# Loading the slopes earlier, holding the decay tables in the shared slots and re-timing the preparation of weights

## The chip, the cores and the metric

One core of a Trainium2 chip runs one launch. The time is device microseconds of that core, the median of several executions. Engines are named as in the profile: PE is TensorE, PEld its weight loads, DVE is VectorE, ACT is ScalarE, POOL is GpSimd, SP is the engine whose queue issues the DMAs.

## The reference

```python
# q, k, v: 4 x 8 heads x 576 x 64
gamma = 1 - 2 ** (-5 - arange(8))
D[i, j] = gamma ** (i - j) if i >= j else 0
x = (((q @ k.T) / 8) * D) @ v            # retention, heads joined: 2304 x 512
h = x @ w_in                             # 512 x 2048
x = (max(h, 0) + alpha * min(h, 0)) @ w_out
out = (sigmoid(x @ w_gate) * (x @ w_val)) @ w_out2   # 512 x 1536, 1536 x 512
```

All of it in float32. `alpha` holds one slope for each of the 2048 hidden columns: 8 KB.

## The kernel before

The 2304 tokens are cut into five blocks (256 and four times 512), and the sequences into 25 runs of up to 128 tokens (chunks); runs 0 and 1 fill block 0, runs 2 to 6 block 1. Each product is made of three matmuls, from operands that are split into a high and a low part (`split`: ACT copies the high part, DVE subtracts).

**Attention.** For each run, POOL multiplies q by a decay table (`att_q`) and v by per-row factors (`att_v`), PE makes the scores `s`, DVE masks them (`sc`, `qk`), PE makes the output `o` and the state update `m`, DVE adds to the state `m_sb`, and ACT and DVE split `o` into `x`. The decay table of a run that does not start a sequence is made by four ACT copies (`dec`, L266) in a pool of two buffers of its own. PE's scores of a run take over the PSUM tiles of an earlier one, so they wait until that one's `x` is split.

**Weights.** A weight block arrives as 64-bit words (`r`, L142, 512 KB), and `prepare_weight` turns it into high and low parts: two ACT rescales (L153, L155), three DVE operations (L159, L160, L163), an ACT copy (L170) and a DVE subtraction (L172). A load is asked for when an earlier block is begun; the first four at the start. `weight_step(n)` adds n to a credit, begins one more weight at each whole credit, and emits one further stage of each weight under way. `PACE_B` is n in the attention runs from `WITH` on, four steps a run; `PACE_C` in the joint steps (L505 to L523), where block 0 and most of block 1 go through the first feed-forward layer, four or five steps for each hidden block f; `PACE_E` in the last block, where the second layer's weights are begun; `PACE_F` in the second layer.

**Slots.** Tiles of 4 KB per partition share a pool of `NSLOT` slots: loaded q, k and v, raw and prepared weights, activations `g`. All 32 weights of the first layer stay until the last block.

**Order.** PE's instructions run in the order written. Those of ACT, DVE, POOL and SP are ordered by a planner that gives each engine the earliest-written instruction that it takes to be ready; on the chip each engine then runs its list in that fixed order. `alpha` is loaded (L481) after the loads of the first seven runs, and L482 makes its negative, `na_sb`, which the slope of the first layer (L410) reads while weights are still being prepared.

The last line of a block of layer 1 (`drain`) copies its four sums from PSUM by way of two staging tiles (`yst`) to HBM; the next block's sums take over the PSUM tiles.

Of the kernel before, what the change touches and what calls it, by code (L numbers as in the profile page):

```python
# [9 lines left out]
F32 = mybir.dt.float32  # L10
# [3 lines left out]
AF = mybir.ActivationFunctionType  # L14
# [4 lines left out]
P = 128  # L19
B, H, S, D = 4, 8, 576, 64  # L20
NPAIR = H // 2
# [5 lines left out]
BLOCKS = (256, 512, 512, 512, 512)  # L27
FIRST = tuple(sum(BLOCKS[:j]) for j in range(len(BLOCKS)))
NBLK = len(BLOCKS)
NSLOT = 38  # L30

ORDER = (1, 2, 3, 4, 0)

# [8 lines left out]

BEHIND = 2

WITH = 3


PACE_B, PACE_C, PACE_E, PACE_F = 0.34, 0.5, 0.65, 1


def chunks():
# [39 lines left out]
def retention_two_ffn(ctx: ExitStack, tc: tile.TileContext, att, cst, alpha, w1, w2, out):  # L91
    nc = tc.nc

    const = ctx.enter_context(tc.tile_pool(name="const", bufs=1))

    big = ctx.enter_context(tc.tile_pool(name="big", bufs=NSLOT))
    xp = ctx.enter_context(tc.tile_pool(name="xp", bufs=2))
# [8 lines left out]
    ap = att_only.enter_context(tc.tile_pool(name="ap", bufs=1))  # L106
    c_sb = ap.tile([P, N_CST], F32, tag="c", name="c_sb")
    al_sb = const.tile([P, NF1], F32, tag="al", name="al_sb")
    na_sb = const.tile([P, NF1], F32, tag="na", name="na_sb")
# [6 lines left out]
    def slot(shape, dtype, name):  # L116
        return big.tile(shape, dtype, tag="big", name=name)
# [66 lines left out]
    def load_weights(n):  # L184
        for key in to_load[:n]:
            load_weight(key)
        del to_load[:n]

    def advance():

        for g in list(under_way):
            if next(g, StopIteration) is StopIteration:
                under_way.remove(g)

    def begin_weight():
        if to_prepare and to_prepare[0] in raw_w:
            under_way.append(prepare_weight(to_prepare.pop(0)))
            load_weights(1)

    def weight(*key):  # L200
        while key not in wt:
            begin_weight()
            advance()
        return wt[key]
# [3 lines left out]
    def weight_step(n):  # L208

        credit[0] += n  # L210
        if credit[0] >= 1.0:
            credit[0] -= 1.0
            begin_weight()
        advance()
# [9 lines left out]
    def load_chunk(n):  # L224
        if n >= len(CHUNKS) or n in raw_a:
            return
        load_qk(n)
        load_kv(n)
# [28 lines left out]
    def att_q(n):  # L257

        _, _, pos, c, _ = CHUNKS[n]
        by = decay  # L260
        if pos:

            by = ap.tile([P, NPAIR, P], F32, tag="dec", name=f"dec{n}", bufs=2)
            for pr in range(NPAIR):
                g = O_GP + STARTS.index(pos) * NPAIR + pr
                nc.scalar.activation(by[:, pr, :c], decay[:, pr, :c], AF.Copy, scale=c_sb[:, g:g + 1])  # L266
        for part in (slice(0, 2), slice(2, 4)) if n == 0 else (slice(0, 4),):
            q = raw_a[n][0][:, 0, part, :c]
            nc.gpsimd.tensor_tensor(out=q, in0=q, in1=by[:, part, :c], op=ALU.mult)  # L269
# [66 lines left out]
    def runs_of(j):  # L336
        return [n for n, ch in enumerate(CHUNKS) if ch[0] == j]
# [6 lines left out]
    def att_stages(j):  # L344

        for n in runs_of(j):
            x_of(n)
            s_sb = att_scores(n, ps_a, "ab")
            load_qk(n + 1)
            yield  # L350
            att_values(n, s_sb, ps_a, "ab")
            load_kv(n + 1)
            if n + 1 < len(CHUNKS):
                att_q(n + 1)
                att_v(n + 1)
            yield

    def att_run(runs, pools, pace, fill):

        scored = []  # L360

        def score(i):
            if i < len(runs):
                n = runs[i]
                x_of(n)
                pool = pools[i % len(pools)]
                scored.append((n, att_scores(n, *pool), *pool))
                if i + 1 < len(runs):
                    att_q(n + 1)
                    att_v(n + 1)  # L370

        def weights(i):
            weight_step(pace(i))
            weight_step(pace(i))

        att_q(runs[0])
        att_v(runs[0])
        score(0)
        for i in range(len(runs)):
            weights(i)  # L380
            att_values(*scored[i])
            fill(i)
            weights(i)
            if i == 0:
                score(1)
            score(i + 2)
# [14 lines left out]
    def ffn1_h(j, f):  # L401
        w = weight(1, f, 0)
        nb = BLOCKS[j]
        ps = ps_h.tile([P, nb], F32, tag="h", name=f"h{j}_{f}")
        products(ps, [(cols(w, k), x_t[j][:, :, k]) for k in range(KC)])
        t = small.tile([P, nb], F32, tag="t", name=f"t{j}_{f}", bufs=1)
        if to_prepare:
            nc.scalar.activation(t, ps, AF.Relu)
            nc.scalar.activation(ps, ps, AF.Relu, scale=-1.0)
            nc.vector.scalar_tensor_tensor(ps, ps, na_sb[:, f:f + 1], t, ALU.mult, ALU.add)  # L410
        else:
            nc.vector.tensor_scalar(t, ps, 0.0, al_sb[:, f:f + 1], ALU.min, ALU.mult)  # L412
            nc.vector.scalar_tensor_tensor(ps, ps, 0.0, t, ALU.max, ALU.add)  # L413
        name = f"g{j}_{f}"
        g_t[j, f] = slot([P, 2, nb], F32R, name) if nb > DM // 2 else half_of_slot(name)
        split(g_t[j, f][:, 0], g_t[j, f][:, 1], ps)
# [31 lines left out]
    def load_x2(j, k):  # L448
        if k == 0:
            x2_t[j] = new_x(j, "x2_")  # L450
        st = small.tile([P, BLOCKS[j]], F32, tag="st", name=f"x2r{j}_{k}")
        nc.sync.dma_start(out=st, in_=x2d[j][:, k, :])
        split(x2_t[j][:, 0, k], x2_t[j][:, 1, k], st)
# [24 lines left out]
    nc.gpsimd.memset(m_sb, 0.0)  # L478
    for n in runs_of(0) + runs_of(1):
        load_chunk(n)  # L480
    nc.sync.dma_start(out=al_sb, in_=alpha)  # L481
    nc.scalar.activation(na_sb, al_sb, AF.Copy, scale=-1.0)  # L482
    load_weights(4)

    pa, py = (ps_a, "ab"), (ps_y, "yy")
# [1 line left out]
    done = [0]  # L487

    def first_h(i):
        while done[0] < EARLY and done[0] * (n0 + n1 - LATE) < EARLY * (i + 1 - LATE):  # L490
            ffn1_h(0, done[0])
            done[0] += 1
# [3 lines left out]
    def later(n):  # L496

        while len(late) > n:
            ffn1_y(*late.pop(0))


    att_run(runs_of(0) + runs_of(1), [pa, py, py], lambda i: PACE_B if i >= WITH else 0, first_h)
    weight(1, 0, 1)

# [19 lines left out]
    n = runs_of(2)[0]  # L524
# [3 lines left out]
    for j in range(1, NBLK):  # L528
        stages = att_stages(j + 1) if j + 1 < NBLK else iter(())
        first = step1 if j == 1 else 0  # L530
        total = 2 * len(runs_of(j + 1))
        span = SPAN * (NF1 - first) // NF1
        staged = 0
        if j == NBLK - 1:
            att_only.close()
            extra.append(ctx.enter_context(tc.tile_pool(name="extra", bufs=NEXTRA)))
        for f in range(first, NF1):
            ffn1_h(j, f)
            if j == NBLK - 1:
                if f == 0:  # L540
                    to_load += [(2, f2, m) for f2 in range(NF2) for m in range(3)]
                    to_prepare += to_load
                    load_weights(3)
                if 8 <= f < 8 + KC:
                    load_x2(ORDER[0], f - 8)
                weight_step(PACE_E)
            for point in range(2):
                if staged < total and staged * span < total * (2 * (f - first) + point):
                    next(stages)
                    staged += 1  # L550
                if point == 0:
                    later(BEHIND - 1)
                    if j == NBLK - 1:
                        weight_step(PACE_E)
            late.append((j, f))
        for _ in stages:
            pass
# [58 lines left out]
```

## Time and profile before

| | |
|---|---|
| median of 3 executions | 947.21 us (946.84 to 948.40) |
| profiled execution | 946.92 us, of which the span of its instructions 945.1 us |
| mean granted TensorE clock | 0.993 |
| busy PE / PEld | 915.4 us (97%) / 769.2 us |
| busy DVE / ACT / POOL | 429.8 / 310.8 / 45.1 us |
| attention runs 0 to 6 | to about 50 us |
| joint steps | about 50 to 155 us |
| rest of layer 1, attention of the other runs | to about 493 us |
| layer 2 | to the end |

In a row of the timeline the first number is the start, the second the duration, `x16` a count of instructions merged, and the bracket holds the engine's idle time before it and what ended it. A granted clock of 1.00 is 2.4 GHz, 0.50 is 1.2 GHz. Times are microseconds from the start of the span.

### The profile page before, as it was taken

Reading aid. Unit: us, or ns where it says so; the run is one execution under the profiler, and the core shown is the slowest. Engines: PE = TensorE matmul, PEld = TensorE weight load, DVE = VectorE, ACT = ScalarE, POOL = GpSimd, SP = SyncE. Lnnn points to the kernel's source line nnn. Section 1 sums busy time; section 2 is a strip of 40 time slices with the busy share of each in tenths; the row PEclk is TensorE's granted clock in tenths of the full one; section 3 lists DMA queues with packets and bytes.
Section 4 is the critical chain, followed back from the end, with each engine's and each line's share of the span. In section 5 each row is a group of like instructions: output and inputs, shape, how many; then the busy total and the mean of one; then the engine's idle time right before and its main releaser. Section 6 shows DMA issues by size and latency. Waiting matters only on the chain.

```text
span 945.1 us, 12323 instructions
## 1 busy us (share of the span) xinstructions
PE 915.4 (97%) x5032; PEld 769.2 (81%) x5032; DVE 429.8 (45%) x726; ACT 310.8 (33%) x604; POOL 45.1 (5%) x46
## 2 busy tenths in 40 slices
PE   6689999999999999999999999999999999999998
PEld 5578888888888888878888888888888888888897
DVE  2989974454443544378787831321122112211212
ACT  3588942221111111157776631211122111211211
POOL 6000001111000000000000000000000000000000
PEclk9799999999999999999999999999999999999999
DMA  9932302332010210145443500200020001000100
GB/s 323 362 100 83 109 23 90 131 103 69 23 57 24 90 45 23 45 160 181 150 155 123 167 1 0 89 1 1 1 74 16 1 1 48 19 1 1 45 1 23
DMA packets 27976, 69.86 MB, mean 74 GB/s; under 512 B 6928, under 2 KB 8464, under 8 KB 27920
## 3 DMA queue, kind: packets, MB, share of 16 engines
q1 hardware_dynamic: 27920, 69.08, 21.6%
q8 instruction: 39, 0.64, 0.3%
q14 instruction: 17, 0.14, 0.0%
HBM read 59.64 MB, written 9.44 MB: 73 GB/s over the span
## 4 chain that ended last, share of the span: by engine, by line
PE 87%; DVE 6%; ACT 3%; DMA 1%; issue 1%; SPq 1%; DVEq 0%; ACTq 0%
PE z L396 31%; PE h L396 18%; PE y L396 17%; PE o L396 16%; PE s L287 1%; DVE r L160 1%; DVE r L163 1%; PE o L326 1%; PE o L306 1%; DVE w L172 1%; ACT r L153 1%; ACT r L155 1%; SPq L253 1%; DMA al_sb<-alpha 1%; DVE h L410 1%
## 5 line engine op out<-in xcount | busy, mean ns | idle before, releaser
L396 PE MATMUL z<-x,w 128*128 128x512 f32 (+1 forms) x1440 | 305.4, 368 | 0.0
L396 PEld LDWEIGHTS z<-x,w 128*128 128x128 f32 x1440 | 252.4, 188 | 45.8
L396 PE MATMUL h<-x,w 128*128 128x512 f32 (+1 forms) x960 | 213.7, 372 | 6.9 <-DVE g L132 5.4
L396 PEld LDWEIGHTS h<-x,w 128*128 128x128 f32 x960 | 167.3, 190 | 39.4 <-DVE g L132 6.4
L396 PE MATMUL y<-g,w 128*128 128x512 f32 x768 | 186.8, 392 | 1.9 <-ACT yst L423 1.9
L396 PEld LDWEIGHTS y<-g,w 128*128 128x128 f32 x768 | 143.2, 188 | 33.4 <-ACT yst L423 2.3
L396 PE MATMUL o<-w,p 128*128 128x512 f32 x648 | 156.8, 389 | 0.0
L463 DVE TENSOR_TENSOR z<-sg,z 128x512 f32<-128x512 f32 (+1 forms) x60 | 38.5, 642 | 258.3 <-PE z L396 258.3
L396 PEld LDWEIGHTS o<-w,p 128*128 128x128 f32 x648 | 120.9, 188 | 24.5
L131 ACT ACTIVATE g<-h 128x512 fp32r<-128x512 f32 (+1 forms) x80 | 44.3, 554 | 199.1 <-DVE h L413 183.0
L462 ACT ACTIVATE sg<-z 128x512 f32<-128x512 f32 (+1 forms) x60 | 33.2, 553 | 169.1 <-PE z L396 168.9
L131 ACT ACTIVATE p<-z 128x512 fp32r<-128x512 f32 (+1 forms) x60 | 33.3, 555 | 132.5 <-DVE z L463 132.5
L412 DVE TENSOR_SCALAR t<-h,al_sb 128x512 f32<-128x512 f32 (+1 forms) x43 | 31.5, 733 | 99.1 <-PE h L396 99.1
L132 DVE TENSOR_TENSOR g<-h,g 128x512 fp32r<-128x512 f32 (+1 forms) x80 | 50.8, 635 | 24.7 <-ACT g L131 22.2
L132 DVE TENSOR_TENSOR p<-z,p 128x512 fp32r<-128x512 f32 (+1 forms) x60 | 38.3, 638 | 33.2 <-ACT p L131 33.1
L160 DVE CUSTOM_DVE_ANT_0 r<-r,t 128x1024 uint16<-128x1024 uint16 x68 | 46.6, 689 | 4.7 <-ACT g L131 0.5
L163 DVE SCALAR_TENSOR_TENSOR r<-r 128x512 uint32<-128x512 uint32 x68 | 46.7, 686 | 0.5
L172 DVE TENSOR_TENSOR w<-r,w 128x512 fp32r<-128x512 f32 x68 | 45.2, 685 | 3.3 <-ACT w L170 3.2
L153 ACT ACTIVATE r<-r 128x512 f32<-128x512 f32 x68 | 45.7, 672 | 1.1 <-DMA r<-w 1.1
L155 ACT ACTIVATE r<-r 128x512 int32<-128x512 uint32 x68 | 45.8, 674 | 0.0
L170 ACT ACTIVATE w<-r 128x512 fp32r<-128x512 f32 x68 | 43.5, 668 | 3.3 <-PE o L396 2.6
L287 PE MATMUL s<-qk 64*128 64x128 f32 (+1 forms) x320 | 24.2, 293 | 10.8 <-POOL qk L269 6.4
(46 smaller groups left out, 506.2 us busy)
## 6 DMA issues: line engine op xcount, KB each, us to landing
r<-w SPq DMA_DIRECT2D x68, 512.0 KB, 3.7
kv<-att SPq DMA_DIRECT2D x16, 512.0 KB, 3.6
qk<-att SPq DMA_DIRECT2D x15, 512.0 KB, 3.9
y<-ost SPq DMA_DIRECT2D x18, 256.0 KB, 2.0
x2d<-yst SPq DMA_DIRECT2D x16, 256.0 KB, 2.3
x2r<-x2d SPq DMA_DIRECT2D x16, 256.0 KB, 2.9
qk<-att SPq DMA_DIRECT2D x6, 256.0 KB, 4.1
kv<-att SPq DMA_DIRECT2D x4, 256.0 KB, 6.2
```

Of the source, the lines that this page charges most:

```text
L131: nc.scalar.activation(hi, src, AF.Copy)
L132: nc.vector.tensor_tensor(out=lo, in0=src, in1=hi.bitcast(F32), op=ALU.subtract)
L153: nc.scalar.activation(high.bitcast(F32), high.bitcast(F32), AF.Copy, scale=2.0 ** -112)
L155: nc.scalar.activation(low.bitcast(I32), low, AF.Copy, scale=2.0 ** -29)
L160: nc.vector.tensor_tensor(out=low.bitcast(I32), in0=low.bitcast(I32), in1=top.bitcast(I32), op=ALU.add)
L163: nc.vector.scalar_tensor_tensor(low, high, 0x80000000, low, ALU.bitwise_and, ALU.bitwise_or)
L170: nc.scalar.activation(w[:, 0, :], low.bitcast(F32), AF.Copy)
L172: nc.vector.tensor_tensor(out=w[:, 1, :], in0=low.bitcast(F32), in1=w[:, 0, :].bitcast(F32), op=ALU.subtract)
L287: nc.tensor.matmul(ps[e][:c, pr, :c], qk[r, 1, pr, :c], qk[r, 0, pr, :c], start=True, stop=True)
L396: nc.tensor.matmul(ps, l, r, start=first and i == 0, stop=last and i == len(todo) - 1)
L462: nc.scalar.activation(t, ps[0], AF.Sigmoid)
L463: nc.vector.tensor_tensor(out=ps[1], in0=t, in1=ps[1], op=ALU.mult)
```

## The change

`alpha` is asked for right after the first run's loads, and its negative is written where the first hidden block of block 0 begins. The decay tables come from the shared slots, which grow from 38 to 39 (two buffers of 2 KB give way to one slot of 4 KB). Weights are begun from the fifth attention run on instead of the fourth, and at 0.62 instead of 0.5 for a step in the joint steps. In the last block of layer 1 the second layer's weights are begun from the third hidden block on; their first three loads stay where they are.

```diff
-NSLOT = 38
+NSLOT = 39
...
-WITH = 3
+WITH = 4
+LATER = 2
-PACE_B, PACE_C, PACE_E, PACE_F = 0.34, 0.5, 0.65, 1
+PACE_B, PACE_C, PACE_E, PACE_F = 0.34, 0.62, 0.65, 1
...
-            by = ap.tile([P, NPAIR, P], F32, tag="dec", name=f"dec{n}", bufs=2)
+            by = slot([P, NPAIR, P], F32, f"dec{n}")
...
     for n in runs_of(0) + runs_of(1):
         load_chunk(n)
-    nc.sync.dma_start(out=al_sb, in_=alpha)
-    nc.scalar.activation(na_sb, al_sb, AF.Copy, scale=-1.0)
+        if n == 0:
+            nc.sync.dma_start(out=al_sb, in_=alpha)
     load_weights(4)
...
     def first_h(i):
+        if i == 0:
+            nc.scalar.activation(na_sb, al_sb, AF.Copy, scale=-1.0)
         while done[0] < EARLY and done[0] * (n0 + n1 - LATE) < EARLY * (i + 1 - LATE):
...
                     load_x2(ORDER[0], f - 8)
-                weight_step(PACE_E)
+                if f >= LATER:
+                    weight_step(PACE_E)
...
                     later(BEHIND - 1)
-                    if j == NBLK - 1:
+                    if j == NBLK - 1 and f >= LATER:
                         weight_step(PACE_E)
```

`first_h(i)` is called behind the output products of run i of the attention (`fill` in `att_run`).

## Rows read from the trace of the kernel before

**Rows 1.** Waits of PE: microseconds in total, times, longest.

```profile
PE h L396 <- DVE g L132: 5.4, 5, 1.9
...
PE o L306 <- DVE m_sb L320: 3.7, 1, 3.7
```

**Rows 2.** Timeline of ACT, 12 to 38 us.

```profile
23.28 0.22 ACT L482 ACTIVATE na_sb<-al_sb 128x16 f32<-128x16 f32 x1 [4.21 <-DMA al_sb<-alpha]
...
24.57 0.64 ACT L153 ACTIVATE r<-r 128x512 f32<-128x512 f32 x1
...
25.67 0.57 ACT L131 ACTIVATE x<-o 128x512 fp32r<-128x512 f32 x1
```

**Rows 3.** Timeline of PE, 12 to 30 us.

```profile
18.69 0.27 PE L326 MATMUL o<-sc,kv 128*64 128x128 f32 x1
...
27.28 0.82 PE L287 MATMUL s<-qk 64*64 64x64 f32 x14 [4.40 <-DVE x L132]
```

**Rows 4.** Timeline of DVE, 14 to 34 us.

```profile
25.24 0.43 DVE L159 TENSOR_SCALAR t<-r 128x512 uint32<-128x512 uint32 x1 [6.24 <-ACT r L153]
...
30.81 0.84 DVE L320 TENSOR_TENSOR m_sb<-m_sb,m 64x256 f32<-64x256 f32 x2
```

**Rows 5.** Timeline of SP's queue, the issues of loads from 16 us on.

```profile
16.52 0.58 SPq L481 DMA_DIRECT2D al_sb<-alpha  x1
17.15 12.39 SPq L142 DMA_DIRECT2D r<-w  x13
```

**Rows 6.** DMA issues at 16.5 and 17.15 us: KB, microseconds from issue to landing.

```profile
al_sb<-alpha SPq DMA_DIRECT2D x1, 8.0 KB, 6.7
...
r<-w SPq DMA_DIRECT2D x1, 512.0 KB, 7.1
```

**Rows 7.** Busy time by stretch, then granted clock, DMA share and GB/s.

```profile
24.57:50.33 25.76, 17.05 (x207) 15.00 (x207) 24.64 (x50) 15.70 (x32) 0.00 (x0) 0.80 0.86 337
50.33:87.00 36.67, 35.51 (x206) 31.31 (x207) 32.64 (x61) 29.69 (x61) 0.00 (x0) 1.00 0.28 90
87.00:113.72 26.72, 24.06 (x156) 21.73 (x155) 26.72 (x53) 24.41 (x51) 0.00 (x0) 1.00 0.34 114
113.72:134.40 20.68, 19.07 (x113) 16.93 (x114) 17.96 (x33) 13.99 (x28) 0.00 (x0) 1.00 0.08 26
```

The columns are the stretch, its length, and the busy time (instructions) of PE, PEld, DVE, ACT and POOL.

**Rows 8.** Timeline of PE at the start of the last block of layer 1.

```profile
419.17 2.07 PE L396 MATMUL y<-g,w 128*128 128x512 f32 x6 [1.89 <-ACT yst L423]
```

**Rows 9.** Busy time by stretch, as in Rows 7, behind that wait.

```profile
420.20:423.60 3.40, 3.40 (x9) 2.63 (x8) 3.40 (x7) 1.90 (x4) 0.00 (x0) 0.50 0.70 220
```

**Rows 10.** Timeline of ACT, 402 to 425 us.

```profile
418.49 0.63 ACT L423 ACTIVATE yst<-y 128x512 f32<-128x512 f32 x1
```

**Rows 11.** Timeline of PE in the joint steps, 122 to 160 us.

```profile
123.60 1.60 PE L396 MATMUL h<-x,w 128*128 128x256 f32 x12
126.81 3.02 PE L396 MATMUL h<-x,w 128*128 128x512 f32 x12 [1.61 <-DVE g L132]
...
133.82 4.35 PE L396 MATMUL h<-x,w 128*128 128x256 f32 x24
...
154.82 2.91 PE L396 MATMUL h<-x,w 128*128 128x512 f32 x12
```

**Rows 12.** Costliest groups of DVE, 25 to 134 us, shapes apart: busy us, mean ns.

```profile
L132 DVE TENSOR_TENSOR g<-h,g 128x256 fp32r<-128x256 f32 x13 | 5.4, 418 | 0.0
```

**Rows 13.** Timeline of SP's queue, 157 to 172 us.

```profile
166.94 0.33 SPq L253 DMA_DIRECT2D kv<-att  x1
```

**Rows 14.** Timeline of PE, 155 to 400 us, scores.

```profile
169.75 1.16 PE L287 MATMUL s<-qk 64*128 64x128 f32 x16
```

**Rows 15.** Timeline of POOL and ACT, 140 to 172 us: a table's use, a table.

```profile
161.89 1.29 POOL L269 TENSOR_TENSOR qk<-qk,dec 128x512 f32<-128x512 f32 x1 [12.26 <-DMA qk<-att]
...
163.22 1.28 ACT L266 ACTIVATE dec<-c_sb 128x128 f32<-128x128 f32 x4 [3.32 <-POOL qk L269]
```

**Rows 16.** Waits of ACT, as in Rows 1.

```profile
ACT r L153 <- DMA r<-w: 1.1, 2, 0.6
```

## The prediction

> **What bounds the kernel now.** I read first the busy shares, then PE's waits, then the timelines of the engines that those waits name, then busy time by stretch. PE is busy 915.4 of 945.1 us, so all that can be had is some 30 us, and they lie in three places.
>
> The first is the attention of the first seven runs. PE stands still for 4.40 us before a run's scores and for 3.7 us before an `o` product [rows 1, 3]. The scores wait for an `x` whose matmuls had ended at 18.69 + 0.27 = 18.96, while ACT copied it only at 25.67 [rows 2, 3]. What is to be seen on ACT: it stood idle 4.21 us in front of `na_sb`, which waited for `alpha`, and behind that came the rescales of the first weight, and only then the `x` [rows 2]. DVE sat idle 6.24 us for the same rescale and did the state update that the `o` product wants at 30.81 [rows 4]. `alpha` was issued at 16.52, right before the first weight's load at 17.15 [rows 5]; they landed 6.7 and 7.1 us later, at 23.2 and 24.25 [rows 6]. So two late landings stand one behind the other in ACT's list, 1 us apart.
>
> The second is the joint steps. From 24.57 to 134.40, where the last weight of layer 1 is ready, DVE works 24.64 + 32.64 + 26.72 + 17.96 = 101.96 of 109.83 us, and from 87.00 to 113.72 all the time [rows 7]. PE's five waits for a `g` (5.4 us) are DVE's lateness [rows 1]. So up to 134 us DVE sets the pace as much as PE.
>
> The third is the start of layer 1's last block: 1.89 us of waiting for a drain [rows 8], behind which the granted clock is at its lower level, 0.50, from 420.2 to 423.6 [rows 9]; half of those 3.4 us is lost, 1.7. The drain itself, on ACT, starts at 418.49 [rows 10], between rescales of the second layer's weights.
>
> **The change part by part.** *Slopes early.* `alpha`'s load moves past twelve loads of SP's queue, six of q and k and six of k and v. Its issue takes 0.58 us [rows 5], so that each could be 0 to 0.58 us late. I take 0: loads wait some 7 us between issue and landing [rows 6], and the queue stays full. The 0.22 us of `na_sb` [rows 2] move to a place where ACT has time, 20 us before its first reader. What does it bring? It takes 4.21 us of idleness from ACT, but the next entry of ACT's list, the first weight's rescale, can't start before 24.25. The weight is written two runs behind the `x` and was put ahead of it all the same; nothing in the change tells the planner that the load will be late, and the start at the fifth run moves the written place, not the landing. If that order stays, the `x` starts at 24.25 + (25.67 - 24.57) = 25.35 instead of 25.67: 0.3 us. The bounds are 0.3 us and, if the attention goes first, all of DVE's 6.24 idle us [rows 4].
>
> *Weights from the fifth run on, and 0.62 a step.* Nothing is added: the same 32 weights, in another order. What the order does is a sum over DVE. Before, sixteen steps of 0.34 begin five weights in the attention (5.44); the other 27 want (27 - 0.44) / 0.5, so 54 joint steps, and three more until the last is ready: the 57th, with the end of hidden block 11. After, twelve steps begin four (4.08); 28 want 27.92 / 0.62, so 46, and three: the 49th, right behind the second product of hidden block 10. So the last weight is ready sooner as PE counts. PE's work between those places is from 123.60 to the end of the first half of the product at 133.82, about 135.3, less a wait of 1.61: 10.1 us [rows 11]. DVE's share in it is the six operations of three activations, at 0.42 us for 256 columns and up to twice that for 512 [rows 12]: 2.5 to 3.4, taken as 2.8.
>
> DVE must do 101.96 - 2.8 = 99.2 us before that place, from 24.57 - 0.3 = 24.3 on, with X idle: 123.5 + X. PE then has 10.1 + (154.82 - 135.3) = 29.6 us without DVE's load to the end of the joint steps, at 153.1 + X, against 154.82. Bounds of X: the 1.1 idle us of the first stretch alone, or all 7.9 [rows 7]. More weights stand ready, which fills the 4.0 idle us from 50.33 to 87.00; of the 2.7 of the last stretch, where weights run out, I keep 1.5. X = 2.6, and the joint steps end 0.9 us later: beginning more weights early only puts more of DVE's work in front of PE's activations, and PE has more left to do when it is over. Bounds -0.6 and +6.2. What hides the weights is PE's own work; where DVE is full that cover is gone, and the activations queued behind a weight's four operations are late next, then PE's next `h`.
>
> *Decay tables in slots.* ACT no longer waits for the table before last, but a table now needs a slot of the shared pool, and asks behind the next run's k and v. Those were issued at 166.94, when the slots of the run before came free at the end of its `o` products [rows 13]; the 39th slot now serves them earlier, and the table takes what comes free at 166.9. The next scores started at 169.75 [rows 14]. In between must lie the `x` copy (0.57), a table (1.28) and POOL's product (1.29) [rows 2, 15]: 166.9 + 3.1 = 170.0, 0.3 us late. That tightness holds for two runs of block 2; the later blocks have more between runs. I take +0.5, bounds 0 and, at 0.4 for each of eleven later tables, 4.4.
>
> *Later start of layer 2's weights.* Three hidden blocks' worth of steps less in front of the drains: the wait of 1.89 and the 1.7 of lower clock go, 3.6 [rows 8, 9]. The loads stay, so rescales can still fill ACT's gaps; bounds 0 and -3.6, taken -3.6. Some 2.6 weights fewer are ready when layer 2 begins, against about 18 that are; that costs nothing.
>
> The sum: +0.9 + 0.5 - 3.6 = -2.2 on the profiled execution's 946.92 (span 945.1 and 1.8 around it), so 944.7; its median over runs is 947.21, 0.3 above, so 945.0. A change below 0.2%, 1.9 us, can't be told from none here.
>
> **The rivals.** *The attention goes first.* With the tables made early and `alpha` there, the planner may put `x`, masks and state updates ahead of the first weight. Then DVE fills its 6.24 us of idleness with some seven operations of 0.6 us, 4.4 us: 940.6. For it: all inputs lie ready at 18.96. Against it: the planner put the weight first with the `x` older. It decides if the `x` precedes L153.
>
> *The joint steps cost more.* If the extra weights don't fill DVE's gaps, X is 7.9: 945.0 + 5.3 = 950.3, slower than before. Its place is `h` behind `g`, 5.4 us before; it decides from about 10 us on. For it: DVE is full already; against it: four of the idle us lie where weights were lacking.
>
> *The drain stays late*, since the first loads and so their rescales are where they were: the change does not do what it says: 945.0 + 3.6 = 948.6. For it: a rescale fills any gap of ACT that the planner sees; against it: the drains are now written ahead of all but those three.
>
> *Tables late in every run:* 945.0 - 0.5 + 4.4 = 948.9; for it the two rows at 166.94 and 169.75, against it the longer spacing later.
>
> *The slot is what lacked.* If PE's waits for `g` came from loads that had no slot, the 39th would give 5.4 us back instead of losing 0.9: 938.7. Against it: ACT waited for a raw weight only 1.1 us in all [rows 16]. The Trainium skill, Perfetto Trace Analysis, "Optimization Strategy", says that a gap repeating on the engine that should be full can mean that the next tile has no room in SBUF or PSUM; by that rule the extra slot would be the gain here, and this trace does not agree, with DVE and not a load named before all five waits.
>
> **How the numbers follow.** Chances: the forecast 0.40 (own range 942.5 to 947.5), attention first 0.19, joint steps dearer 0.17, drain late 0.12, tables late 0.08, slot 0.04. Faster, below 945.3, takes 0.22 of the forecast, all but 0.01 of the second case and the slot: 0.44. Slower, above 949.1, takes 0.01 of the forecast, 0.13 of the third case, 0.05 of the drain's and 0.04 of the tables': 0.23. The rest, 0.33, is the same. The range 938.5 to 950.5 leaves out the far tails of the second and the third, where idle time of both ends meets the other terms' bounds, less than 0.2.
>
> **What would show it.** In the new trace: no wait of ACT for `alpha`, but one for the first weight, with the `x` behind it near 25.4 (or near 19, then the second case); the joint steps' end near 155.7 and `h` behind `g` above 6 us; DVE full from 50 to 110; no wait for a drain in the last block and a clock of 1.00 around it; scores in block 2 a few tenths late. I am wrong if the order on ACT turns, or if PE waits for DVE little in spite of a full DVE.

## The result, and the profile after

The changed kernel takes 955.49 us (median of 4, 954.09 to 955.91) against 947.81 for the kernel before, run beside it: ratio 1.0084 (95% interval 1.0070 to 1.0098), 7.7 us slower. The profiled execution, the quickest of the four, took 954.09 us, its span 952.3. Lines of the changed kernel are two further on (L396 is L398), L410 to L413 included; the copy of a `yst` is L425 and `na_sb` L493.

Where the time goes is read best as a race between the two traces, by the start of the same PE instruction:

| PE starts | before | after | later by |
|---|---|---|---|
| first `h` of block 0 | 42.36 | 43.09 | 0.7 |
| second product, hidden block 0 (`y0a`) | 55.7 | 56.6 | 0.9 |
| the same, hidden block 4 | 85.3 | 88.0 | 2.7 |
| hidden block 6 | 97.5 | 105.8 | 8.3 |
| hidden block 9 | 119.3 | 130.7 | 11.4 |
| end of the joint steps (`h`) | 154.82 | 164.36 | 9.5 |
| layer 2 | 493.0 | 500.2 | 7.2 |
| end | 945.1 | 952.3 | 7.2 |

So most of the loss is made between 85 and 130 us; 1.9 us come back by the end of the joint steps and some 2.4 more before layer 2. PE's waits after, as in [rows 1] (microseconds in total, times, longest):

```profile
PE s L289 <- POOL qk L271: 10.1, 5, 5.4
PE h L398 <- DVE g L134: 7.8, 5, 3.5
PE o L308 <- DVE m_sb L322: 5.9, 2, 3.9
PE h L398 <- ACT w L172: 2.2, 2, 1.8
PE h L398 <- DVE w L174: 0.9, 2, 0.6
```

PE waits 7.8 us for a `g` instead of 5.4, and newly 3.1 us for weights (`w`). The wait of 4.4 us for an `x` [rows 3] is down to 0.3 and the one for a `yst` [rows 8] is gone. But the waits for POOL's `qk` grew from 6.4 to 10.1 us and those for the state `m_sb` from 4.3 to 5.9, so the attention ends no sooner for it. The start, on ACT's timeline, as in [rows 2]:

```profile
8.40 0.22 ACT L493 ACTIVATE na_sb<-al_sb 128x16 f32<-128x16 f32 x1 [6.39 <-DMA al_sb<-alpha]
8.52 4.80 ACT L268 ACTIVATE dec<-c_sb 128x128 f32<-128x128 f32 x17
...
23.91 0.67 ACT L155 ACTIVATE r<-r 128x512 f32<-128x512 f32 x1 [9.40 <-DMA r<-w]
...
26.04 0.70 ACT L155 ACTIVATE r<-r 128x512 f32<-128x512 f32 x1 [0.90 <-DMA r<-w]
...
27.18 0.61 ACT L133 ACTIVATE x<-o 128x512 fp32r<-128x512 f32 x1
```

The slopes' negation is now the first entry of ACT's list; it waits 6.39 us for `alpha` and holds the tables until 8.52. Later the first weight's rescale stands in front of the `x`, as forecast, but a second weight's rescale does too: the `x` is copied at 27.18, not 25.35. PE's timeline in the joint steps, three of its eight rows with a wait, as in [rows 11], and then the busy time by stretch, as in [rows 7] and [rows 9]:

```profile
59.96 0.50 PE L398 MATMUL h<-x,w 128*128 128x256 f32 x2 [1.78 <-ACT w L172]
...
97.67 5.49 PE L398 MATMUL h<-x,w 128*128 128x512 f32 x12 [3.32 <-DVE g L134]
...
123.53 4.60 PE L398 MATMUL h<-x,w 128*128 128x512 f32 x12 [3.50 <-DVE g L134]
```

```profile
50.33:87.00 36.67, 33.99 (x190) 29.50 (x189) 31.12 (x58) 29.88 (x61) 0.00 (x0) 0.98 0.27 95
87.00:113.72 26.72, 23.20 (x125) 20.13 (x124) 26.72 (x53) 23.27 (x47) 0.00 (x0) 0.87 0.30 99
113.72:133.30 19.58, 16.08 (x97) 14.39 (x96) 17.68 (x33) 13.85 (x28) 0.00 (x0) 0.91 0.08 28
...
96.29:103.12 6.83, 5.45 (x13) 4.34 (x14) 6.83 (x15) 6.47 (x13) 0.00 (x0) 0.50 0.29 100
...
123.60:127.00 3.40, 3.40 (x8) 2.70 (x9) 3.40 (x8) 0.95 (x2) 0.00 (x0) 0.50 0.00 0
```

The twelve matmuls that follow each of the two long waits take 5.49 and 4.60 us; twelve such took 3.02 before [rows 11]. Around both, the granted clock is 0.50, the lower of its two levels (1.2 GHz), where before it was 1.00 all through the joint steps [rows 7]. DVE is full from 87 to 113.72 (26.72 of 26.72), and from 50 to 87 idle for 5.55 us, more than the 4.03 of before.

### The profile page after: what moved, and what is told of

Read it like the earlier page. It is cut to its first block, busy times and chain, and to the rows that moved or that the text cites. A ratio compares the mean times of both kernels' runs of the same rounds, so it can differ in the third digit from the quotient of the medians.

```text
span 952.3 us, 12300 instructions
## 1 busy us (share of the span) xinstructions
PE 920.5 (97%) x5032; PEld 773.0 (81%) x5032; DVE 433.3 (45%) x729; ACT 308.3 (32%) x598; POOL 44.5 (5%) x46
## 4 chain that ended last, share of the span: by engine, by line
PE 88%; DVE 3%; ACT 2%; DMA 2%; issue 2%; SPq 1%; POOL 0%; POOLq 0%; DVEq 0%; ACTq 0%
PE z L398 31%; PE h L398 19%; PE y L398 16%; PE o L398 15%; DMA r<-w 2%; PE s L289 1%; PE o L328 1%; PE o L308 1%; PE m L314 1%; PE y0b L398 1%; PE y0a L398 1%; DVE r L165 1%; SPq L255 1%; ACT r L155 1%; DMA kv<-att 1%
## 5 line engine op out<-in xcount | busy, mean ns | idle before, releaser
L398 PE MATMUL z<-x,w 128*128 128x512 f32 (+1 forms) x1440 | 305.3, 368 | 0.0
L398 PEld LDWEIGHTS z<-x,w 128*128 128x128 f32 x1440 | 252.3, 188 | 45.9
L398 PE MATMUL h<-x,w 128*128 128x512 f32 (+1 forms) x960 | 218.0, 378 | 10.9 <-DVE g L134 7.8
L398 PEld LDWEIGHTS h<-x,w 128*128 128x128 f32 x960 | 170.3, 193 | 44.6 <-DVE g L134 9.0
L398 PE MATMUL y<-g,w 128*128 128x512 f32 x768 | 186.4, 392 | 0.0
L398 PEld LDWEIGHTS y<-g,w 128*128 128x128 f32 x768 | 143.3, 188 | 31.6 <-ACT g L133 0.9
L398 PE MATMUL o<-w,p 128*128 128x512 f32 x648 | 156.8, 389 | 0.0
L398 PEld LDWEIGHTS o<-w,p 128*128 128x128 f32 x648 | 120.9, 188 | 24.6
L289 PE MATMUL s<-qk 64*128 64x128 f32 (+1 forms) x320 | 24.4, 295 | 10.4 <-POOL qk L271 10.1
```

The costliest lines, as they stand in the source:

```text
L289: nc.tensor.matmul(ps[e][:c, pr, :c], qk[r, 1, pr, :c], qk[r, 0, pr, :c], start=True, stop=True)
L398: nc.tensor.matmul(ps, l, r, start=first and i == 0, stop=last and i == len(todo) - 1)
```

## The experiments

All medians are compared with the kernel before as run beside them (946.7 to 947.4 us).

**Each part by itself.** The later start: `if f >= LATER` on the kernel before.

> The kernel before with the later start of the second layer's weights alone. If the prediction's term stands (the wait of 1.89 us for a drain and 1.7 us of lower clock go, nothing is late in their place), it is 3.6 us faster, near 944.0, and the granted clock stays at 1.00 around the start of layer 1's last block. If the 5 steps left out only move a rescale to another drain or leave layer 2 short of weights, it is within 1 us of before, and a wait of PE for a second layer's weight or for a drain shows in its place.

Measured: 945.42 against 947.05 us, ratio 0.9985 (0.9975 to 0.9996), 1.6 us faster. In the profiled execution, the quickest of its twelve (943.25), no wait for a `yst` is left, and PE is busy all through the stretch where 1.89 us were lost before, at full clock:

```profile
410.00:440.00 30.00, 29.98 (x132) 24.21 (x131) 22.69 (x39) 21.97 (x41) 0.00 (x0) 1.00 0.55 193
```

That one span is 3.6 us shorter, the forecast number, but this is the luck of one execution; the median gives 1.6. The mechanism holds; of its size, less than half is measured.

```diff
-PACE_B, PACE_C, PACE_E, PACE_F = 0.34, 0.5, 0.65, 1
+PACE_B, PACE_C, PACE_E, PACE_F = 0.34, 0.62, 0.65, 1
```

> The kernel before with 0.62 in place of 0.5 weights begun in a joint step, and nothing else. Theory A, the pace is what cost: more of DVE's and ACT's work stands in front of the activations, PE waits for a g and the clock falls behind each long wait, as in the changed kernel at 96 and 123 us; then it is 4 to 9 us slower, the joint steps end near 160, and PE shows waits of over 3 us for a g. Theory B, the prediction's sum for the pace was right and the loss came from the start of the kernel: the time is within 1.5 us of before and the joint steps end at 154 to 156.

Measured: 953.27 against 947.05, ratio 1.0066 (1.0053 to 1.0079), 6.2 us slower. Theory A. The joint steps end at 162.98, 8.2 us late. PE's timeline, the two longest of its four waits for a `g` and the product behind the first of them:

```profile
95.77 5.49 PE L396 MATMUL h<-x,w 128*128 128x512 f32 x12 [2.72 <-DVE g L132]
101.06 3.32 PE L396 MATMUL y<-g,w 128*128 128x512 f32 x12
...
122.15 4.60 PE L396 MATMUL h<-x,w 128*128 128x512 f32 x12 [3.31 <-DVE g L132]
```

Two stretches of it, columns as in [rows 7]:

```profile
88.00:106.00 18.00, 15.28 (x80) 13.21 (x80) 17.45 (x34) 15.58 (x31) 0.00 (x0) 0.81 0.27 89
106.00:124.00 18.00, 14.58 (x88) 12.84 (x87) 17.01 (x33) 13.80 (x29) 0.00 (x0) 0.95 0.18 60
```

The 8.2 us can be added up: the first `h` is 0.6 late; the waits for a `g` are 8.0 us instead of 5.4, 2.6 more; and the lower clock costs 4.5: the products took 5.49 and 4.60 us where twelve such took 3.02 [rows 11], and 3.32 where the kernel before took 2.88 (at 94.75). That is 7.7; the other 0.5 is not resolved here. (The mean clock of a stretch would give more, 5.2 us, because it also counts time in which PE stood still.) What the wait of 3.31 us is made of shows on DVE's timeline. A `g` needs L410 and then L132; between them the planner's list holds four operations of weights and a fifth:

```profile
118.81 0.48 DVE L410 SCALAR_TENSOR_TENSOR h<-h,na_sb,t 128x256 f32<-128x256 f32 x1
119.21 0.68 DVE L172 TENSOR_TENSOR w<-r,w 128x512 fp32r<-128x512 f32 x1
119.81 0.42 DVE L159 TENSOR_SCALAR t<-r 128x512 uint32<-128x512 uint32 x1
120.14 0.68 DVE L163 SCALAR_TENSOR_TENSOR r<-r 128x512 uint32<-128x512 uint32 x1
120.75 0.68 DVE L172 TENSOR_TENSOR w<-r,w 128x512 fp32r<-128x512 f32 x1
121.35 0.42 DVE L159 TENSOR_SCALAR t<-r 128x512 uint32<-128x512 uint32 x1
121.68 0.41 DVE L132 TENSOR_TENSOR g<-h,g 128x256 fp32r<-128x256 f32 x1
```

From the start of L410 to the start of L132 are 2.87 us, of which L410 itself needs 0.48. ACT's copy of the same `g` lies between the two as well: it ran from 119.95 to 120.34, behind two rescales of a weight in ACT's list. So the 0.7 us in front of that copy are ACT's lateness, and the 1.3 us behind it are DVE's. Before, the pair was 1.66 us apart:

```profile
111.58 0.48 DVE L410 SCALAR_TENSOR_TENSOR h<-h,na_sb,t 128x256 f32<-128x256 f32 x1
...
113.24 0.42 DVE L132 TENSOR_TENSOR g<-h,g 128x256 fp32r<-128x256 f32 x1
```

```diff
-NSLOT = 38
+NSLOT = 39
...
-            by = ap.tile([P, NPAIR, P], F32, tag="dec", name=f"dec{n}", bufs=2)
+            by = slot([P, NPAIR, P], F32, f"dec{n}")
```

> The kernel before with the decay tables in slots and 39 slots, and nothing else. By the prediction: 0 to 1 us slower, 0.3 us of it in block 2's two runs. Rival: the two tables that block 2's runs read, made early on an idle ACT before, can't be made before their slot, so ACT's list has two weights' rescales in front of the second x; then that x is copied near 27 instead of 25.67, and the joint steps end 1 to 4 us late, with the tables' 2.5 us of ACT's time added between 140 and 185 us.

Measured: 950.73 against 947.05, ratio 1.0041 (1.0026 to 1.0055), 3.7 us slower: the rival. On ACT two weights' rescales precede the `x`, which is copied at 27.60; on GpSimd (POOL) the `q` products of runs 1 and 2 come behind the `v` products of both, so that the third run's scores wait too:

```profile
15.75 3.47 PE L287 MATMUL s<-qk 64*128 64x128 f32 x32 [3.16 <-POOL qk L269]
...
128.98 4.50 PE L396 MATMUL h<-x,w 128*128 128x512 f32 x12 [2.24 <-DVE g L132]
```

The first `h` is 1.5 us late and the joint steps end 3.7 us late; in between lies a product at the lower clock, the second row. The profiled execution is the slowest of the six, its span 5.4 us longer than before: two waits of 0.3 us for a `qk` in block 2 and 1.0 us more of waiting for a drain (2.9 instead of 1.9) make up most of the rest.

The slopes: `alpha` behind the first run's loads, `na_sb` in `first_h`, and nothing else.

> The kernel before with the slopes' load after the first run's and their negation written in the first run, and nothing else. The negation now stands behind two decay tables in ACT's list and in front of the third. By the prediction: 0.3 us faster at most, nothing late. Rival: the load lands near 8.4 us, ACT waits for it, the third run's table and the scores behind it come 1 to 3 us late; of that 0.5 to 2.5 us reach the end if the attention has no slack, and nothing if the first weight's landing near 24 us sets the pace all the same.

Measured: 946.84 against 947.05, ratio 0.9999 (0.9991 to 1.0008). No change, for a reason that neither theory named. ACT's timeline:

```profile
8.28 0.21 ACT L491 ACTIVATE na_sb<-al_sb 128x16 f32<-128x16 f32 x1 [2.00 <-DMA al_sb<-alpha]
...
23.81 1.28 ACT L266 ACTIVATE dec<-c_sb 128x128 f32<-128x128 f32 x4 [4.17 <-POOL qk L269]
...
26.10 0.58 ACT L131 ACTIVATE x<-o 128x512 fp32r<-128x512 f32 x1
```

The 4.21 us of waiting for `alpha` [rows 2] have become 4.17 us of waiting for GpSimd: the table that stood behind `na_sb` in the list waits for a buffer of its ring, which the product of the last run of block 1 frees.

**Is it DVE's load?** The operation at L163, which joins the sign into a weight, is left out of the kernel before, at a pace of 0.5 and of 0.62:

```diff
-        nc.vector.scalar_tensor_tensor(low, high, 0x80000000, low, ALU.bitwise_and, ALU.bitwise_or)
```

> The kernel before without one of the four vector operations on a weight, the one that joins in the sign (0.68 us each, 32 of them in the joint steps, 21.9 us of DVE's work); its output lacks the signs. It is the mate of the next run, to be compared with it. If DVE's load sets the pace of the joint steps, the waits of PE for a g (5.4 us in five before) nearly vanish and the time falls by 4 to 8 us; if the order of ACT's and the loads' work sets it, it falls by less than 2.

> The same lighter weights with 0.62 in place of 0.5. Theory A, DVE's load in front of the activations is what made 0.62 cost 6 us: with 21.9 us of it gone, 0.62 is within 2 us of its mate, and no wait for a g is longer than 2 us and the granted clock stays at 1.00 from 60 to 130 us. Theory B, the cost is in ACT's list (four operations of a weight in front of the activations there) or in slots: 0.62 costs 5 to 7 us with the lighter weights too.

Measured: 938.11 and 941.45, against 946.68: ratios 0.9904 (0.9890 to 0.9918) and 0.9941 (0.9928 to 0.9953). Taking 0.68 us from each weight is worth 8.6 us at 0.5. In the profile the joint steps end 6.0 us sooner (148.79): 2.7 us of that are won ahead of the first second product (52.95), 3.3 by shorter waits for a `g`; the rest comes later. So DVE's load does set the pace, in the joint steps and in the attention ahead of them. The higher pace then costs 3.3 us instead of 6.2: neither theory's number. The profiles say which part went. Waits for a `g`, first at 0.5, then at 0.62:

```profile
PE h L395 <- DVE g L132: 2.1, 5, 0.9
```

```profile
PE h L395 <- DVE g L132: 5.0, 5, 1.6
```

The waits grow by 2.9 us, as they did with the full load (2.6), but none is longer than 1.6, and the granted clock is 1.00 from 42 to 145 us in both. The part of the lower clock is gone, the part of the waits is still there.

**Which order do the slots upset?** The third run's kernel, with GpSimd's instructions in the written order, as PE's are:

```diff
-        with tc.manual_schedule(engines={mybir.EngineType.PE}):
+        with tc.manual_schedule(engines={mybir.EngineType.PE, mybir.EngineType.Pool}):
```

> The tables in slots alone, as in the third run, but with GpSimd's work in the written order, so that a run's q product again precedes the next run's v product. Theory A, the order on GpSimd is what the slots cost: the wait of 3.2 us in front of the third run's scores goes, the first h is back near 42.4 us (43.9 with slots alone), the joint steps end near 155 to 156, and 2 to 4 of the 3.7 us are won back. Theory B, the cost comes from ACT, which has two weights' rescales in front of the second x: then the x is still copied near 27.6 and the joint steps end near 158 all the same.

Measured: 952.71 against 946.68, ratio 1.0058 (1.0043 to 1.0072), 6.0 us slower: theory A fails. The wait of 3.16 us is gone, yet the first `h` starts at 43.74, where it started at 43.88 with slots alone. The second `x` is copied at 27.46, and the scores behind it wait 8.6 us for it. The joint steps end at 156.76, between the two expectations. So the order on GpSimd is not what holds the `x` and the first `h`. What the trace shows in front of them is ACT's list, with two rescales ahead of the `x`; no run held that list's order fixed.

**Weights from the fifth run on:** `WITH = 4` alone.

> The kernel before with weights begun from the fifth run on in place of the fourth, and nothing else. What the other parts leave of the whole: the four parts measured sum to +8.1 us (6.2 + 3.7 - 1.6 - 0.2) of +8.4, so 0 to 1 us slower if parts add. By the prediction's sum one weight less begun in the attention puts the last weight two joint steps later: within 1 us. Rival: the first weights are late for the first joint steps, PE waits for a weight near 47 and 60 us (2.2 us in the changed kernel) and the time is 2 to 3 us longer, and another part gives it back in the whole.

Measured: 949.79 against 946.68, ratio 1.0031 (1.0019 to 1.0042), 3.1 us slower: the rival. PE's timeline, two of its rows:

```profile
46.23 0.50 PE L396 MATMUL h<-x,w 128*128 128x256 f32 x2 [0.57 <-ACT w L170]
...
58.92 0.50 PE L396 MATMUL h<-x,w 128*128 128x256 f32 x2 [1.78 <-ACT w L170]
```

Two stretches, columns as in [rows 7]:

```profile
42.00:80.00 38.00, 34.56 (x224) 30.25 (x223) 30.54 (x57) 25.61 (x53) 0.00 (x0) 0.96 0.27 95
80.00:145.00 65.00, 61.36 (x361) 54.15 (x360) 58.64 (x111) 50.34 (x103) 0.00 (x0) 0.97 0.22 74
```

The attention ends 0.8 us sooner (first `h` at 41.54), but the first joint steps find their weights not ready, and the clock is below 1.00 in both stretches.

**Parts taken out of the whole.** The changed kernel with the pace at 0.5, and with the tables in their ring (`NSLOT` 38):

> The changed kernel with the pace of the joint steps back at 0.5. If 0.62 costs beside the other parts what it costs alone, 6.2 us, it takes 949.3 against 955.5, and the low clock between 96 and 127 us goes. Rival: beginning weights later in the attention makes the first weights late and the higher pace catches up for it, so that the parts don't add (6.2 + 3.7 + 3.1 - 1.6 - 0.2 = 11.2, where the whole is 8.4); then taking the pace back wins 2 to 4 us only, 951.5 to 953.5.

> The changed kernel with the decay tables back in their ring of two and 38 slots. If the slots cost 3.7 us beside the other parts as they do alone, 951.8 us, with ACT's second x copied near 26 in place of 27.2 and the first h at 42.0 to 42.5 in place of 43.1. If they cost only what they do after the joint steps or at the last block's start, which the later start of layer 2's weights covers here, 954 to 955.

Measured: 949.58 and 955.33, against 947.12: ratios 1.0034 (1.0021 to 1.0048) and 1.0081 (1.0068 to 1.0094). Without the higher pace the excess falls from 7.7 to 2.5 us; the pace is worth 5.2 of it in the whole, nearly what it costs alone. One product at the lower clock is left (4.62 us, behind a wait of 2.15 that ended at 116.38). Without the slots the excess stays at 8.2: in the whole the slots cost nothing. The ring does bring the first `h` forward, from 43.09 to 42.44, but PE then waits longer for DVE:

```profile
PE h L398 <- DVE g L134: 9.2, 4, 4.3
```

That is 1.4 us more than with slots. The first `h` of a single execution is a weak measure, though: in five kernels whose lists of ACT, DVE and POOL are the same up to 40 us (before, the later start, 0.62, and the paces of 0.42 and 0.56 below) it comes anywhere from 41.90 to 43.43.

Two more runs, the slots and `WITH = 4` on the kernel before, and the changed kernel with `WITH = 3`:

> The kernel before with the tables in slots and with weights from the fifth run on, these two alone. If the slots' cost in the attention lies under the wait for the late first weights, the two together cost 3.5 to 5 us; if they add, 6.8.

> The changed kernel with weights from the fourth run on again. If beginning them at the fifth run costs its 3.1 us here too (the waits for weights near 47 and 60 us, 3.1 us in the profile, and the lower clock behind them), 952 to 953. If the slots' cost then comes out from under it, 954.5 to 956, and the waits for weights are replaced by waits for the second x and the state.

Measured: 952.79 and 951.93, against 947.40: ratios 1.0057 (1.0035 to 1.0079) and 1.0044 (1.0032 to 1.0057). Together the two cost 5.4 of a sum of 6.8, between the two expectations. In the whole, `WITH = 4` costs 3.2 of 7.7 us. With `WITH = 3` the waits for weights are gone and the waits for a `g` grow to 9.6.

**How the cost grows with the pace.** 0.56 alone, and 0.42 with the later start:

> The kernel before with 0.56 weights begun in a joint step. If the cost grows evenly with the pace (6.2 us for 0.12), 3 us slower, near 950. If it sets in where a wait for a g becomes longer than about 2 us and the granted clock falls behind it, either within 1 us of before with the clock at 1.00 in the joint steps, or 4 to 6 us slower with a stretch at 0.50.

> The kernel before with the later start of layer 2's weights and 0.42 weights begun in a joint step in place of 0.5. If fewer weights in front of the activations mean shorter waits for a g, the waits fall below 4 us and the time is 1 to 3 us under the later start alone (945.4), 942.5 to 944.5. If 0.42 is too slow, PE waits for weights in the last third of the joint steps and it takes 946 to 950.

Measured: 948.75 against 947.40, ratio 1.0011 (1.0000 to 1.0022); 942.78 against 947.12, ratio 0.9956 (0.9943 to 0.9968), which is 4.3 us faster and 2.7 more than the later start alone. At 0.56 the cost is less than even growth would give, and yet the clock falls once; at 0.42 the first expectation holds.

| pace | change of the time by the pace | waits for a `g` in total, longest | granted clock 88 to 145 us |
|---|---|---|---|
| 0.42 | -2.7 | 2.7, 1.0 | 1.00 |
| 0.50 | 0 | 5.4, 1.9 | 1.00 |
| 0.56 | +1.4 | 7.1, 2.2 | 0.91 in 106 to 124 |
| 0.62 | +6.2 | 8.0, 3.3 | 0.81, 0.95, 0.96 |

Each step up adds waits, and from 0.56 on lower clock. At 0.42 PE waits 0.9 us for a weight of a first product near the end (at 143.7), which suggests a floor close by.

**A version that beats both.** From the fourth and the second run's lessons: the first two weights' loads go ahead of the last three runs' loads, with the slopes early and the later start; then the same with 0.42.

```diff
         load_chunk(n)
+        if n == 3:
+            load_weights(2)
         if n == 0:
             nc.sync.dma_start(out=al_sb, in_=alpha)
-    load_weights(4)
+    load_weights(2)
```

> The kernel before with the slopes early, the later start of layer 2's weights, and the first two weights' loads put ahead of the last three runs' loads, so that their rescales are done while ACT idles. If the second x's place behind late landings is what holds the attention (the wait of 4.4 us for it, and 3.7 us for the state behind it), the x is copied before 22 us, the first h starts 3 to 5 us sooner than 42.4, and the time is 2 to 5 us under 945.4. Rival: the last three runs' loads, 2.4 us later, or DVE's weight operations in front of the third run's masks take it back: within 1 us of 945.4.

> The twelfth run's kernel (slopes early, later start, first two weights' loads ahead) with 0.42 weights begun in a joint step. If its gain (4.8 us) and that of 0.42 over the later start alone (2.7 us) add, it is 7 us faster than before, 939 to 940.5. If the last weights become late for the joint steps, which now begin 1.6 us sooner, it stays at 942 to 943.

Measured: 942.31 against 947.12, ratio 0.9949 (0.9936 to 0.9962); 940.18 against 947.40, ratio 0.9922 (0.9901 to 0.9942). The second is 7.2 us faster than before, near the sum of 4.8 and 2.7. The first is faster by the amount expected, but not in the way: its second `x` comes at 25.11, not before 22, because the second weight's ACT copy stands in front of it and waits 2.11 us for DVE; the first `h` is only 0.1 us sooner, and 1.6 are won by the first second product (54.1 against 55.7). With 0.42 the waits for a `g` fall from 5.2 to 2.2 us. Its first `h` is at 40.26, but those 2 us are not the pace's doing: up to 40 us the lists of ACT, DVE and POOL are the same as in the first, and what differs is the granted clock (0.84 against 0.99 from 30 to 40 us).

## Why the prediction was wrong

It forecast 945.0, in 938.5 to 950.5; 955.5 is outside, on the other side of no change.

**The pace and the fifth run: this step failed.** It forecast the joint steps' end 0.9 us late; they end 9.5 us late. Its place for the last weight and its sum of DVE's work were right. The last weight is ready with the 49th step (last subtraction at 131.38 to 133.3, hidden block 10's second product at 133.58), and DVE's work up to there is 24.41 + 31.12 + 26.72 + 17.68 = 99.9 us from 23.91 on, against a forecast of 99.2. X, DVE's idle time, was put at 2.6 with a bound of 7.9; it is 133.3 - 23.91 - 99.9 = 9.5: 2.0 up to 50.33, 5.55 up to 87.00, none up to 113.72 and 1.9 behind it. From the forecast end of 155.7, that is 6.9 us; the start of the sum took off 0.4, DVE's work added 0.7, and PE's rest was 31.1 us instead of 29.6: 164.4. The sentence that failed is "more weights stand ready, which fills the 4.0 idle us from 50.33 to 87.00". With the pace alone they do fill it (36.06 of 38 us busy from 50 to 88, against 33.97 before). In the whole the first weights are begun a run later; PE waits for them, DVE waits for PE, and from 50.33 to 87.00 the 5.55 us stay idle. In the changed kernel with `WITH = 3`, DVE is busy for 34.70 of the 36.67 us, so it is the fifth run that leaves it idle. The prediction costed the fifth run only as a shift of the last weight and not the lateness of the first ones; alone that is worth 3.1 us.

Read from PE instead of DVE (the same time once more, not to be added), the larger omission was the clock. The step priced waits at their length. With the pace alone and in the whole, the two longest waits for a `g` are followed by products at 0.50, and of the 8.2 us that the pace alone costs in the joint steps about 4.5 are lower clock, 2.6 waits. The changed kernel with `WITH = 3` bears this out: it has the pace, and waits for a `g` of 9.6 us, but a clock of 1.00, and from the first `h` to the end of its joint steps are 115.6 us, 3.2 more than before; with the pace alone they are 7.6 more. The prediction had used just this price in the last block [rows 9] and did not carry it to PE's waits for DVE.

**Rivals.** "The joint steps cost more" had the right mechanism and place, `h` behind `g`, with X at its bound of 7.9, where 9.5 was measured; 950.3 was short by what the late first weights and the clock behind the waits add. The rule of the Trainium skill (Perfetto Trace Analysis, "Optimization Strategy"), that a repeating gap can mean too little room for the next tile, was rightly set aside: with the 39th slot the waits for a `g` grew from 5.4 to 7.8 us and name DVE each time, and taking the slot and the tables back leaves the time as it is. No run adds a slot by itself.

**Slopes early:** 0.3 us was forecast, 0.2 measured, which is within the uncertainty of none, and the list did not go as described. On the kernel before, a table's wait for its ring took `alpha`'s place; in the whole, two rescales and not one precede the `x`. "A place where ACT has time" was wrong as well: the negation became ACT's first entry and held the tables from 3.81, where they started before, to 8.52. The forecast sign "no wait of ACT for `alpha`" failed with it.

**Slots:** +0.5 was forecast for block 2 and up to 4.4 for later blocks. Block 2 came out as forecast: in the changed kernel two of its scores wait 0.3 us each for a `qk`, where none waited before. But alone the slots cost 3.7, most of it for another reason: the tables leave the ring, and ACT's list is put together anew, in the attention. This is read from the traces; no run isolates it. In the whole that cost does not show. A reading that fits, but is not shown, is that DVE's queue sets the end of the joint steps there: in the profile without slots an attention that ends 0.65 us sooner is followed by 1.4 us more of waiting for DVE. The late first weights explain 1.4 of the 3.7 us at most. What brings the planner to put two rescales ahead is open, and so is why executions of one kernel differ by 2 to 5 us (949.71 to 952.33 with the slots alone, 948.87 to 954.18 in the changed kernel at 0.5).

**Later start:** -3.6 was forecast. What is left out are two hidden blocks' steps, four in all, which at 0.65 are the prediction's 2.6 weights; its "three hidden blocks' worth" and the "5 steps" of the first expectation are miscounted. In the changed kernel no wait for a drain is left, and from 410 to 440 us PE is busy all the time at 1.00:

```profile
410.00:440.00 30.00, 30.00 (x133) 24.59 (x132) 18.68 (x30) 13.93 (x25) 0.00 (x0) 1.00 0.36 114
```

Before, that start cost 1.89 us of waiting and 1.7 of clock [rows 8, 9]. From the joint steps to layer 2 the changed kernel is only 2.4 us quicker, so 1.2 are lost elsewhere on the way (0.6 of it are the two waits in block 2), and alone the term measures -1.6 by the median.

The parts alone add up to 6.2 + 3.7 + 3.1 - 1.6 - 0.2 = 11.2, the whole is 7.7; the difference is about what the slots no longer cost.

## What to carry to other kernels

When a second engine is full, starting its background work sooner puts it in front of the work that the first engine waits for: look at what stands between the two operations of one activation in that engine's list, and price it per wait, with the clock behind the wait. Before taking away a wait at the head of a list, read the next entries and what each of them waits for; the same 4 us may be there again. A part that costs 3.7 us alone can cost nothing in the whole and the other way round, so undo parts from the whole as well as adding them to the old kernel.

## What the runs showed of the hardware that was not expected

The length of a wait alone does not tell whether PE's clock falls behind it. In the kernel before, a wait of 1.93 us that ended at 113.72 left it at 1.00 [rows 7]. A wait of 2.24 us (slots alone, above) was followed by twelve matmuls that took 4.50 us instead of 3.02, and so was one of 2.16 at the pace of 0.56, on PE's timeline:

```profile
118.29 4.61 PE L396 MATMUL h<-x,w 128*128 128x512 f32 x12 [2.16 <-DVE g L132]
```

Waits of one length can end either way. With the slopes alone, a wait of 1.95 us that ended at 114.15 was followed by twelve matmuls in 3.02 us. With the slots and GpSimd in the written order, a wait of 1.95 us was followed by twelve in 4.62, on PE's timeline:

```profile
114.28 4.62 PE L396 MATMUL h<-x,w 128*128 128x512 f32 x12 [1.95 <-DVE g L132]
```

And in the changed kernel with `WITH = 3`, waits of 2.72 and 3.32 us did not bring the lower clock. Its PE timeline, and behind it the busy time by stretch, with the granted clock at 1.00:

```profile
96.46 3.06 PE L398 MATMUL h<-x,w 128*128 128x512 f32 x12 [2.72 <-DVE g L134]
...
121.03 3.02 PE L398 MATMUL h<-x,w 128*128 128x512 f32 x12 [3.32 <-DVE g L134]
```

```profile
80.00:145.00 65.00, 57.38 (x344) 50.77 (x343) 55.31 (x106) 41.60 (x84) 0.00 (x0) 1.00 0.20 66
```

What decides between these cases no run here shows.
